# A convolution and soft mixture of experts on one core, rewritten: 64x64 tiles, block transposes on VectorE, and x in two halves

## The chip, the cores and the metric

The kernel runs on one core of a Trainium2 chip. The core has a matrix engine (TensorE, PE in the profile), a vector engine (VectorE, DVE), a scalar engine (ScalarE, ACT), GpSimd (POOL), and queues that start DMA transfers: SyncE's (SP) and, if a kernel uses it, ScalarE's. Inputs and output lie in HBM; the engines work on SBUF (128 partitions), and TensorE writes to PSUM (8 banks of 512 fp32 numbers per partition).

The metric is the device time of one execution in microseconds (us). Lower is better.

## The reference

Everything is fp32. With `x` of shape (8, 3584, 192), `weight` (8 heads, 7 taps), `phi` (192, 32), `w1` (8, 192, 1024) and `w2` (8, 1024, 192):

```python
w = softmax(weight)                       # per head, over the 7 taps
y[b, s, h, g] = sum_k w[h, k] * x_pad[b, s + k, h, g]   # causal, 6 zero rows in front, 24 channels a head
y = y.reshape(28672, 192)                 # N tokens
logits = y @ phi                          # (N, 32): 8 experts x 4 slots
d = softmax(logits over the N tokens)     # dispatch weights
slot_input = d.T @ y                      # (32, 192)
slot_out[e] = relu(slot_input[e] @ w1[e]) @ w2[e]       # 4 slots per expert
c = softmax(logits over the 32 slots)     # combine weights
out = c @ slot_out                        # (N, 192)
```

The dispatch softmax runs over all tokens, so no output row can be computed before all tokens have been read once. That makes three phases: convolution, logits and the sums over tokens; the experts; the combine. x is 22.0 MB, w1 and w2 are 6.3 MB each, the output is 22.0 MB.

## The kernel before, in words

**Tokens** are cut in two ways. Eleven "P" chunks hold tiles of 120 consecutive tokens on partitions. `conv_p` (matmul at L551) multiplies windows of 128 rows with a band matrix `toep` of 128 x 120, one matmul of 384 columns per head and 16 tiles; the result is copied from PSUM (banks `cv0`, `cv1`) to `xc` by ACT through the helper `copy` (L231 is its ACT branch, L233 its DVE branch). Four "D" chunks (the first 2048 tokens of four batches) hold 16 consecutive tokens per partition, loaded with a halo of 6 tokens as rows of 16.9 KB. `conv_d` convolves them without TensorE: ACT does the first tap (L589), DVE the other six of each head (L599).

**`stage_b`** takes each chunk through TensorE transposes (L634, L653; copied to `xt1`, `xt2`), logits in four column groups of 32 (L668, L672), the running maximum (L689, L694), logits turned back with tokens on partitions (L709), subtraction and exponential (L735, L763), and the dispatch product with four column groups (L790). Its sums are rescaled by the change of the maximum (L702) and accumulated in `sacc` (L817, L810). `epath` computes the combine softmax in `eall` per token (L833 to L849).

**Experts.** Sums of groups are merged (L1037), the first layer is L1083 and L1087, the ReLU L1097, the transposes L1107, the second layer L1129. Late w1 and w2 loads reuse buffers of x. The upper 64 rows of w1 are loaded two experts at a time onto 128 partitions (L907, `w1[2 * q : 2 * q + 2, P:D, :]`).

**Combine.** The weights are split in a high and a low part (L994), transposed in pairs of tiles (L1008), and multiplied with `st`, which is split likewise, in fp32r (L1187). `store` sends the result to HBM, P tiles as rows of 768 B (L1216), D chunks as rows of 6 KB (L1204).

**Order.** All steps are given to `Plan` with their reads, writes, costs and priorities. It list-schedules them over the engines by these costs and emits each engine's instructions in that order. All DMAs are issued from SP, in one order, and SP waits at an issue until its buffer is free:

```python
src = bass.AP(x.tensor, (b * S + s0 - HALO) * D, ap=[[D, P], [M * D, e - i], [1, D]])
nc.sync.dma_start(xv[:, i:e, :], src)
```

Of the kernel before, what the change touches and what calls it, by code (L numbers as in the profile page):

```python
# [10 lines left out]
F32R = mybir.dt.float32r  # L11
# [6 lines left out]
class Plan:  # L18
    """Collects steps in program order with the buffers they read and write, orders them by list
    scheduling over the engines (every dependency between two steps is kept), then emits them."""  # L20

    LAG = {"PE": 0.22, "ACT": 0.2, "DVE": 0.16, "DMA": 2.1, "POOL": 0.2}
    SELF = {"PE": 0.0, "ACT": 0.1, "DVE": 0.12, "DMA": 2.1, "POOL": 0.1}
    SWITCH = 0.15
    FILL = 1500.0
    SLIP = 0.05
    LOOK = {"PE": 0.05, "ACT": 0.12, "DVE": 0.12, "DMA": 0.0, "POOL": 0.0}

    def __init__(self):
        self.steps = []  # L30
        self.urgent = 0.0
        self.writer = {}
        self.readers = {}

    def add(self, fn, cost, reads=(), writes=(), prio=0.0, bias=0.15):
        i = len(self.steps)
        deps = set()
        for r in reads:
            if r in self.writer:
                deps.add(self.writer[r])  # L40
        for w in writes:
# [9 lines left out]
        self.steps.append((fn, cost, deps, prio, bias, self.urgent))  # L51
        return i

    def list_order(self, todo, out):
        n = len(self.steps)
        succ = [[] for _ in range(n)]
        miss = [len(s[2]) for s in self.steps]
        for i, s in enumerate(self.steps):
            for d in s[2]:
                succ[d].append(i)  # L60
        ready = [i for i in range(n) if miss[i] == 0 and i in todo]
        free = {e: 0.0 for e in self.LAG}
        est = [{e: 0.0 for e in s[1]} for s in self.steps]
        busy = {e: 0.0 for e in self.LAG}
        while ready:
            best = None
            for e in free:
                cands = []
                for i in ready:
                    cost = self.steps[i][1]  # L70
                    if e not in cost:
                        continue
                    s = max(free[e], est[i][e])
                    if len(cost) > 1:
                        f = s + cost[e] - (self.SWITCH if e == "ACT" else self.steps[i][4])
                        if any(max(free[o], est[i][o]) + cost[o] < f for o in cost if o != e):
                            continue
                    cands.append((s, i))
                if not cands:
                    continue  # L80
                lim = min(cands)[0]
                s, i = min(
                    ((s, i) for s, i in cands if s <= lim + max(self.LOOK[e], self.steps[i][5])),
                    key=lambda c: (self.steps[c[1]][3], c[1]),
                )
                key = (s, busy[e], i, e)
                if best is None or key < best:
                    best = key
            s, _, i, e = best
            busy[e] += self.steps[i][1][e]  # L90
            ready.remove(i)
            f = s + self.steps[i][1][e]
            free[e] = f
            out.append((s, i, e))
            for k in succ[i]:
                for o in est[k]:
                    lag = self.SELF[e] if o == e else self.LAG[e]
                    est[k][o] = max(est[k][o], f + lag)
                miss[k] -= 1
                if miss[k] == 0 and k in todo:  # L100
                    ready.append(k)
        return est, miss, succ

    def order(self):
        """First the steps that phases 1 and 2 wait for, by list scheduling; the others go into the gaps."""
        n = len(self.steps)
        out = []
        est, miss, succ = self.list_order({i for i in range(n) if self.steps[i][3] < self.FILL}, out)
        assert len(out) == sum(s[3] < self.FILL for s in self.steps)
        done = {i for _, i, _ in out}  # L110
        held = {e: sorted((t, t + self.steps[i][1][e]) for t, i, x in out if x == e) for e in self.LAG}
        ready = {i for i in range(n) if i not in done and miss[i] == 0}
        busy = {e: 0.0 for e in self.LAG}

        def fit(e, i):
            t, c, h = est[i][e], self.steps[i][1][e], held[e]
            k = max(0, bisect.bisect_left(h, (t, 0.0)) - 1)
# [5 lines left out]
        fits = {}  # L123
        while ready:
            best = None
# [1130 lines left out]
```

## Time and profile before

| | |
|---|---|
| median of 3 runs | 317.65 us (315.68 to 321.15) |
| span of the profiled execution | 314.0 us, first to last instruction |
| median less that span | 3.65 us |
| instructions | 5852 |
| TensorE clock granted, mean | 0.916 of full speed |
| moved by DMA | 60.55 MB, mean 193 GB/s |

The profile is of one execution. Its page gives busy time per engine, the span in 40 slices (a digit is the busy share in tenths), the chain of work that ended last, and groups of instructions by source line. A group's line reads: line, engine, operation, output<-input, shapes, count | busy us, mean ns of one | idle time before it and what ended it. A stage's line reads: from:to in us, length, then busy us (and instructions) of PE, PE weight loads, DVE, ACT and POOL, then the granted TensorE clock, the DMA share and GB/s. A line of the chain reads: start, us, what. A line of a timeline is the same with the engine's name; SPq is the queue of SP. PEld is TensorE loading weights. Busy time counts overlapping instructions of one group once.

### The profile page before, as it was taken

The page shows a single profiled execution, that of the slowest core. Times are in us where ns is not written, and L with a number is a line of the kernel's source. Part 1 is how long each engine was busy: PE and PEld are TensorE (multiplying, and loading weights), DVE is VectorE, ACT ScalarE, POOL GpSimd, SP SyncE. Part 2 cuts the span into 40 slices and gives each one's busy share as a digit, 9 for nine tenths or more (in the row PEclk, how much of TensorE's full clock was granted, in tenths as well). Part 3 has the DMA queues.
Part 4 walks back from the last instruction along what each step waited for, and adds up shares of the span by engine and source line. Part 5 has one row for each costly group of instructions (what it writes and reads, how often), then busy time and mean ns, then how long its engine had stood idle before and what let it go on. Part 6 is the DMA issues. An engine that isn't in the chain of part 4 may idle for free.

```text
span 314.0 us, 5852 instructions
## 1 busy us (share of the span) xinstructions
PE 251.1 (80%) x2189; PEld 173.9 (55%) x2189; DVE 216.6 (69%) x497; ACT 196.9 (63%) x468; POOL 10.5 (3%) x48
## 2 busy tenths in 40 slices
PE   5467979996999899999400699989999999897700
PEld 5233454564456456665200466655689999887600
DVE  3616597996999899999910078888899997821100
ACT  2365678684878698756400385664379997786620
POOL 6000000100010000000000000020000000000000
PEclk9596799999999999999855599999999999999975
DMA  6999997997039654311372951980039989899995
GB/s 185 205 257 210 235 327 277 243 232 204 1 97 275 157 153 140 106 51 54 102 163 82 365 167 45 316 243 2 2 105 253 296 228 313 259 259 305 299 317 186
DMA packets 55909, 60.55 MB, mean 193 GB/s; under 512 B 2154, under 2 KB 52810, under 8 KB 55370
## 3 DMA queue, kind: packets, MB, share of 16 engines
q1 hardware_dynamic: 55882, 60.19, 67.7%
q8 instruction: 17, 0.28, 0.4%
q14 instruction: 10, 0.08, 0.1%
HBM read 38.16 MB, written 22.02 MB: 192 GB/s over the span
## 4 chain that ended last, share of the span: by engine, by line
PE 42%; DMA 36%; DVE 6%; SPq 6%; ACT 3%; issue 1%; ACTq 0%; DVEq 0%
DMA xd<-in_x_dram 14%; DMA x<-in_x_dram 11%; DMA out_dram<-xc 11%; PE cv L551 9%; PE tr L634 5%; SPq L477 5%; DVE xcd L599 4%; PE sp L790 4%; PE cv L1187 3%; PE lt L668 3%; PE lt L672 2%; PE tr L653 2%; PE tr L1008 2%; PE sp L1129 2%; ACT xc L231 1%
## 5 line engine op out<-in xcount | busy, mean ns | idle before, releaser
L599 DVE SCALAR_TENSOR_TENSOR xcd<-xd,wb,xcd 128x384 f32<-128x384 f32 x192 | 105.2, 615 | 9.6 <-ACT xcd L589 9.3
L551 PE MATMUL cv<-x,toep 128*120 128x384 f32 x160 | 67.5, 531 | 33.8 <-DMA x<-in_x_dram 31.6
L231 ACT COPY xc<-cv 120x384 f32<-120x384 f32 (+3 forms) x132 | 58.2, 476 | 55.5 <-PE cv L551 47.2
L551 PEld LDWEIGHTS cv<-x,toep 128*120 128x120 f32 x160 | 26.5, 195 | 57.3 <-issue 40.0
L231 ACT COPY xt<-tr 128x480 f32<-128x480 f32 (+2 forms) x104 | 48.2, 514 | 13.4 <-PE tr L634 9.7
L689 DVE TENSOR_SCALAR_CACHE_REDUCE lts<-lt 128x480 f32<-128x480 f32 (+2 forms) x15 | 9.9, 657 | 31.6 <-PE lt L672 31.5
L634 PEld LDWEIGHTS tr<-ident,xc 120*128 120x128 f32 x172 | 19.6, 144 | 15.1 <-ACT xt L231 6.8
L634 PE MATMUL tr<-ident,xc 120*128 120x120 f32 x172 | 24.1, 277 | 4.3 <-ACT xt L231 4.3
L1187 PE MATMUL cv<-st,et 128*120 128x192 f32 (+1 forms) x160 | 21.7, 276 | 3.2 <-ACT xc L231 1.8
L589 ACT ACTIVATE xcd<-xd,wb 128x384 f32<-128x384 f32 x32 | 19.0, 648 | 7.8 <-DMA xd<-in_x_dram 7.8
L1187 PEld LDWEIGHTS cv<-st,et 128*120 128x120 f32 (+1 forms) x160 | 18.8, 187 | 4.4 <-ACT xc L231 2.2
L1008 PE MATMUL tr<-ident,xd 120*128 120x120 f32 (+1 forms) x118 | 17.3, 270 | 0.0
L790 PE MATMUL sp<-xc,dsb 120*32 120x193 f32 x344 | 16.3, 329 | 0.9 <-ACT dsb L763 0.9
L231 ACT CAST et<-tr 128x480 fp32r<-128x480 f32 (+1 forms) x26 | 15.4, 596 | 2.2 <-PE tr L1008 2.2
L668 PE MATMUL lt<-xt,phi 128*32 128x480 f32 (+2 forms) x120 | 16.0, 607 | 0.0
L672 PE MATMUL lt<-xt,phi 128*32 128x480 f32 (+2 forms) x120 | 15.9, 602 | 0.0
L790 PEld LDWEIGHTS sp<-xc,dsb 120*32 120x32 f32 x344 | 10.3, 109 | 7.6 <-ACT dsb L763 2.8
L1187 PE MATMUL lt<-st,et 128*120 128x192 f32 (+1 forms) x80 | 12.4, 278 | 2.5 <-ACT xc L231 1.9
L735 DVE TENSOR_TENSOR dsb<-ln,mbs 120x512 f32<-120x512 f32 (+2 forms) x16 | 9.6, 613 | 6.3 <-ACT mbs L231 6.1
L233 DVE CAST xd<-eall 120x256 fp32r<-120x256 f32 (+2 forms) x24 | 7.0, 290 | 9.5 <-PE tr L1008 9.4
L1008 PEld LDWEIGHTS tr<-ident,xd 120*128 120x128 f32 (+1 forms) x118 | 12.3, 140 | 1.5 <-issue 1.2
L994 DVE TENSOR_TENSOR xd<-eall,xd 120x256 fp32r<-120x256 f32 (+2 forms) x30 | 12.6, 418 | 0.7
(154 smaller groups left out, 407.4 us busy)
## 6 DMA issues: line engine op xcount, KB each, us to landing
x<-in_x_dram SPq DMA_DIRECT2D x14, 768.0 KB, 28.8
out_dram<-xc SPq DMA_DIRECT2D x13, 720.0 KB, 9.8
xd<-in_x_dram SPq DMA_DIRECT2D x4, 1848.0 KB
out_dram<-xc SPq DMA_DIRECT2D x8, 768.0 KB, 6.2
x<-in_moe_w_dram SPq DMA_DIRECT2D x4, 768.0 KB
w1a<-in_moe_w_dram SPq DMA_DIRECT2D x5, 512.0 KB, 8.8
xd<-in_moe_w_dram SPq DMA_DIRECT2D x4, 512.0 KB
out_dram<-xc SPq DMA_DIRECT2D x4, 450.0 KB
```

The source lines that it names most:

```text
L231: nc.scalar.copy(dst, src)
L477: nc.sync.dma_start(xv[:, i:e, :], src)
L551: nc.tensor.matmul(pv, toep[:, h, :], ch["x"][:, 0:nt, d0:d1], start=True, stop=True)
L589: nc.scalar.activation(o, xv[:, 0:nt, d0 : d0 + CG], AF.Copy, scale=wb[:, h * KT : h * KT + 1])
L599: nc.vector.scalar_tensor_tensor(out=o, in0=xv[:, k : k + nt, d0 : d0 + CG], scalar=wb[:, h * KT + k : h * KT + k + 1], in1=o, op0=ALU.mul ...
L634: nc.tensor.transpose(tv[:, g, 0:R], src, ident[0:R, 0:R])
L668: nc.tensor.matmul(lv[g * NS : (g + 1) * NS], phi1, v1[:, 0:C, g, 0:R], start=True, stop=False)
L672: nc.tensor.matmul(lv[g * NS : (g + 1) * NS], phi2[g % 2], v2[:, 0:C, g // 2, 0:R], start=False, stop=True)
L790: nc.tensor.matmul(ps["sp"][g * NS : (g + 1) * NS, 0:D1], dsb[0:R, c, g * NS : (g + 1) * NS], mv, start=(c == 0), stop=(c == C - 1),)
L994: nc.vector.tensor_tensor(out=eh.bitcast(F32R)[0:R, 0:n, 1, :], in0=ev, in1=eh[0:R, 0:n, 0, :], op=ALU.subtract)
L1008: nc.tensor.transpose(tv[:, i, 0:R], eh[0:R, 2 * i : 2 * i + 2, :, :].rearrange("p t a n -> p (t a n)"), ident[0:R, 0:R])
L1187: nc.tensor.matmul(po[0:R, u, 0:D], et[:, i, 0:R], st[u][v], start=(v == 0), stop=(v == 1))
```

## The change

The kernel is written anew; phases and mathematics stay.

- **Tokens:** each batch is 64 windows of 56 tokens, 32 in each half of the partitions. A window is 64 rows (6 of the window before it, two beyond its end). All tokens go through TensorE; the convolution by DVE and the D chunks are gone.
- **x** has two buffers `xs` of one batch each. The lower half is issued by SP, the upper half by ACT.
- **`conv`:** the band matrix is 64 x 64 on both halves; a head is four matmuls of 384 columns, one per 64x64 tile of the array, into two banks. One ACT copy of 768 elements per head moves it to `xc`.
- **`chain`:** six DVE transposes in 32x32 blocks (1024 elements each) make `xt`; 96 matmuls of 32x32 tiles (256 or 192 columns) make the logits of the batch in four banks; DVE takes the maximum and transposes the logits back (`tin`); ACT takes the exponential; eight PE transposes, two ACT copies, the dispatch product, the accumulation with the correction `al`.
- **`rows`** is the combine softmax, now with two passes and one sum on POOL. **`slots`** transposes the weights back with DVE into the freed `xc`.
- **Experts:** one fp32 pass as before; the weights' last 64 rows are loaded onto 64 partitions at a time (`w1b`); `w1a` has a buffer of its own, `w1b` and `w2` reuse `xs` and `xt`.
- **Combine:** plain fp32, contraction over 32 rows in four row groups, into four banks; evictions of up to 768 elements by ACT or DVE. Each partition holds 7 consecutive tokens of a quarter of a batch, so a store sends 5376 B per partition (1536 B and 768 B in the first batch).
- **`Plan`** is shortened: a list schedule for the first two phases, then the rest into the gaps.

The core of the new code:

```diff
+    def load_x(b):
+        def src(row0, rows, win0, wins):
+            return bass.AP(x.tensor, (base + T * win0 + row0) * D, ap=[[D, rows], [T * D, wins], [1, D]])
+        def low(e):
...
+            nc.sync.dma_start(xv[0:64, 1:NW, :], src(0, 64, 1, NW - 1))
+        def high(e):
+            if b < B - 1:
+                nc.scalar.dma_start(xv[64:128, :, :], src(0, 64, NW, NW))
...
+        add(low, dma(n), reads=[f"z{s}"], writes=[f"xs{s}l"], prio=b * 10 - 30)
+        add(high, dma(n), writes=[f"xs{s}h"], prio=b * 10 - 30)
...
+    def conv(b):
...
+            def mm(e, h=h, k=k):
+                for g in range(2):
+                    for hf in range(2):
+                        r = slice(64 * hf, 64 * hf + 64)
+                        nc.tensor.matmul(
+                            cv[k][64 * g : 64 * g + 64, hf, 0 : NI * CG].rearrange("p (i c) -> p i c", c=CG),
+                            toep[r, h, :],
+                            xs[s][r, g::2, h * CG : (h + 1) * CG],
+                            start=True, stop=True,
+                        )
...
+            add(ev, {"ACT": act(2 * NI * CG)}, reads=[f"cv{k}", "one"], writes=[xck[s][h]], prio=pr)
...
+    def chain(b):
...
+            def tr(e, k=k):
+                nc.vector.transpose(xt[:, k], xc[s][:, :, 1 + 32 * k : 33 + 32 * k])
...
+            def lmm(e, k=k):
+                for a in range(4):
+                    r = slice(32 * a, 32 * a + 32)
+                    n = 24 if a % 2 else 32
+                    for c in range(4):
+                        nc.tensor.matmul(
+                            lg[32 * c : 32 * c + 32, a, 0 : U * n].rearrange("p (u j) -> p u j", j=n),
+                            phi4[r, k, :],
+                            xt[r, k, U * c : U * c + U, 0:n],
+                            start=(k == 0), stop=(k == NB - 1), tile_position=(32 * a, 32 * c),
+                        )
...
+                nc.vector.tensor_reduce(out=nmr[:, b, odd : odd + 1], in_=lview(odd), axis=AX.XY, op=ALU.max, negate=True)
...
+                nc.scalar.activation(
+                    dT[:, :, odd::2, 0:n].rearrange("p u a j -> p a u j"),
+                    lview(odd).rearrange("p a (u j) -> p a u j", j=n), AF.Exp, bias=nm,
+                )
+            def tin(e, odd=odd, n=n, q0=q0):
+                nc.vector.transpose(
+                    eall[:, b, q0 : q0 + n // 2, :].rearrange("p (a k) m -> p a (k m)", a=2), lview(odd)
+                )
...
+            def disp(e, v=v):
+                for u in range(4 * v, 4 * v + 4):
+                    for c in range(4):
+                        nc.tensor.matmul(
+                            lg[32 * c : 32 * c + 32, 2, 0:D1], dn[:, u, 32 * c : 32 * c + 32], xc[s][:, U * c + u, :],
+                            start=(u == 0), stop=(u == U - 1),
+                        )
...
+    load_x(0)
+    load_x(1)
+    conv(0)
+    for b in range(B):
+        chain(b)
+        if b + 2 < B:
+            load_x(b + 2)
+        if b + 1 < B:
+            conv(b + 1)
...
+        load_w(
+            w1b[64 * a : 64 * a + 64], w1[a::2, P:D, :].rearrange("q p f -> p q f"), P * F * 8,
+            f"w1b{a}", ["xs0l", "xs0h"], 1020 + a,
+        )
...
+            def mm(e, qs=qs, banks=banks, cb=cb, k=k):
+                for q in qs:
+                    for c in range(4):
+                        r = slice(32 * c, 32 * c + 32)
+                        nc.tensor.matmul(
+                            banks[c][:, (q - k) * D : (q - k + 1) * D], cb[r, :, q], so[r, :],
+                            start=True, stop=True, tile_position=(32 * c, 0),
+                        )
...
+                    dst = bass.AP(out.tensor, (b * S + c * NQ) * D, ap=[[TQ * D, P], [1, TQ * D]])
+                    nc.sync.dma_start(dst, ob[:, c].rearrange("p q d -> p (q d)"))
-                        nc.vector.scalar_tensor_tensor(
-                            out=o,
-                            in0=xv[:, k : k + nt, d0 : d0 + CG],
-                            scalar=wb[:, h * KT + k : h * KT + k + 1],
-                            in1=o,
```

More of the change, by code (lines that the diff above doesn't have):

```diff
@@ L1 @@
-import bisect
 from contextlib import ExitStack
@@ L50, in add, with order @@
         deps.discard(i)
[L51 to L55, printed above, removed]
+        self.steps.append((fn, cost, deps, prio))
+    def order(self):
+        S = self.steps
+        n = len(S)
         succ = [[] for _ in range(n)]
-        miss = [len(s[2]) for s in self.steps]
-        for i, s in enumerate(self.steps):
+        for i, s in enumerate(S):
             for d in s[2]:
                 succ[d].append(i)
[L61 to L94, printed above, removed]
-            for k in succ[i]:
[L96 to L102, printed above, removed]
@@ L104, in order @@
-    def order(self):
-        n = len(self.steps)
-        out = []
[L108 to L117, printed above, removed]
+        prio = [s[3] for s in S]
@@ L164, in order @@
+        run({i for i in range(n) if prio[i] < self.FILL}, False)
+        done = {i for _, i, _ in out}
+        run({i for i in range(n) if i not in done}, True)
         assert len(out) == n
         out.sort()
-        self.end = max(b for h in held.values() for _, b in h)
-        self.trace = [(s, e, self.steps[i][1][e], self.steps[i][3]) for s, i, e in out]
         return out
@@ new lines, in tile_conv_softmoe, with selector @@
+    add(c1, {"POOL": 3.0}, writes=["one", "dT", "s1z", "s2z", "z1"], prio=-90)
+    add(lambda e: nc.gpsimd.memset(hz, 0.0), {"POOL": 2.2}, writes=[f"hz{q}" for q in range(4)], prio=-20)
+    def phi_load(e):
+        for a in range(4):
+            nc.sync.dma_start(phi4[32 * a : 32 * a + 32], phi.rearrange("(k p) n -> p k n", p=32))
+    add(phi_load, {"DMA": 0.5}, writes=["phi4"], prio=-25)
+    def selector(e):
+        nc.vector.tensor_reduce(out=gsel[:, 0:NS], in_=ident.rearrange("p (g n) -> p n g", n=NS), axis=AX.X, op=ALU.add)
@@ new lines, in tile_conv_softmoe, with merge @@
+    for b in range(B):
+        rows(b)
+    for b in range(B):
+        slots(b)
+    pr = 300
+    pv4 = lambda t: t.rearrange("p (q a i) -> p q a i", a=2, i=SPE)
+    nmf = nmr[:, B, 2:3]
+    add(
+        lambda e: nc.tensor.matmul(cv[0][:, 0, 0:P], nmf.broadcast_to((P, P)), ident, start=True, stop=True),
+        {"PE": 0.25}, reads=[f"nm{B - 1}", "ident"], writes=["cv0"], prio=75.5,
+    )
+    def merge(e):
+        nc.vector.tensor_reduce(
+            out=gmin, in_=cv[0][:, 0, 0:P].rearrange("p (g n) -> p n g", n=NS), axis=AX.X, op=ALU.min
+        )
+        nc.vector.tensor_tensor(out=gtmp, in0=gmin, in1=gsel[:, 0:NS], op=ALU.mult)
+        nc.vector.tensor_reduce(out=gcol, in_=gtmp, axis=AX.X, op=ALU.add)
@@ L1126, in l2 @@
+                    copy(e, hz[:, 2 * q : 2 * q + 2, x_, x_ * SPE : (x_ + 1) * SPE], tv[:, :, c_ : c_ + SPE])
+            return fn
+        add(hcopy(0), {"DVE": 0.4}, reads=[f"ht{q % 2}", f"hz{q}"], writes=[f"hz{q}a"], prio=pr + 3)
+        add(hcopy(1), {"ACT": 0.8}, reads=[f"ht{q % 2}", f"hz{q}"], writes=[f"hz{q}b"], prio=pr + 3)
+        op = lg[:, 2, 0:D]
+        def l2(e, q=q):
+            for j in range(2):
                 for a in range(2):
@@ new lines, in l2 @@
+                            start=(q == 0 and j == 0 and a == 0), stop=(q == 3 and j == 1 and a == 1),
+                        )
+        add(
+            l2, {"PE": 1.4}, reads=[f"hz{q}a", f"hz{q}b"] + [f"w2.{e}" for e in range(E)],
+            writes=["op"], prio=pr + 1.5,
+        )
+    add(
+        lambda e: nc.vector.tensor_scalar(out=os_, in0=op, scalar1=ri, scalar2=None, op0=ALU.mult),
+        {"DVE": 0.35}, reads=["op", "ri"], writes=["os"], prio=pr + 4,
+    )
+    add(
+        lambda e: nc.tensor.matmul(lg[:, 3, 0:D], gsel, os_, start=True, stop=True),
+        {"PE": 0.35}, reads=["os", "gsel"], writes=["lg1"], prio=pr + 4,
+    )
```

1223 lines of the change are left out of this document (377 added, 846 removed).

## The prediction

> **What bounds the kernel now.** I read the page from the top: the span, the busy shares, then the forty slices, because a mean over stages hides which engine sets each.
>
> ```profile
> span 314.0 us, 5852 instructions
> ...
> PE 251.1 (80%) x2189; PEld 173.9 (55%) x2189; DVE 216.6 (69%) x497; ACT 196.9 (63%) x468; POOL 10.5 (3%) x48
> ...
> DMA  6999997997039654311372951980039989899995
> ```
>
> No engine is full over the span, and the DMA row has a hole from the 10th slice to the 30th and is full again at the end. So I asked for stages (busy time of PE, weight loads, DVE, ACT, POOL; clock, DMA share, GB/s).
>
> ```profile
> 80.00:100.00 20.00, 20.00 (x167) 11.18 (x166) 19.93 (x42) 16.24 (x37) 1.36 (x3) 1.00 0.48 118
> 100.00:120.00 20.00, 18.96 (x174) 11.60 (x173) 18.41 (x39) 16.36 (x40) 0.00 (x0) 1.00 0.54 150
> 130.00:140.00 10.00, 10.00 (x107) 6.03 (x108) 9.97 (x22) 7.00 (x18) 0.12 (x1) 1.00 0.13 53
> 160.00:180.00 20.00, 4.58 (x18) 3.38 (x19) 0.00 (x0) 2.02 (x4) 0.00 (x0) 0.52 0.70 211
> 240.00:248.00 8.00, 8.00 (x78) 8.00 (x77) 7.76 (x21) 7.78 (x19) 0.00 (x0) 1.00 0.97 315
> 296.00:302.00 6.00, 1.92 (x16) 1.75 (x16) 0.00 (x0) 3.54 (x9) 0.00 (x0) 1.00 0.99 360
> 302.00:310.00 8.00, 0.00 (x0) 0.00 (x0) 0.00 (x0) 0.00 (x0) 0.00 (x0) 0.50 0.94 282
> ```
>
> Three limits follow one another. From 80 to 140 us PE and DVE are both full while DMA is half idle or worse: compute sets the pace. From 130 the queue moves only 53 GB/s at a share of 0.13, two engines of sixteen: the four late loads of w1, whose access pattern begins with a dimension of 2. The x behind them in the same queue is late, and from 160 to 180 everything waits for it. From 240 on the stores fill the DMA. The end of the chain of waits shows the three parts:
>
> ```profile
> 213.45 0.43 DVE saccD L810
> 222.28 1.44 PE sp L1129 x32
> 230.19 1.16 PE cv L1187 x7
> ```
>
> Sums over tokens end at 213.9, experts until 230.2 (16.3 us), combine until 314 (84 us).
>
> **The change, part by part.**
>
> *What goes.* The convolution by DVE, its largest group, and the PE transposes for the logits with their ACT evictions:
>
> ```profile
> L599 DVE SCALAR_TENSOR_TENSOR xcd<-xd,wb,xcd 128x384 f32<-128x384 f32 x192 | 105.2, 615 | 9.6 <-ACT xcd L589 9.3
> L231 ACT COPY xt<-tr 128x480 f32<-128x480 f32 x63 | 33.2, 570 | 8.0 <-PE tr L634 7.2 <-PE tr L653 0.7
> ```
>
> DVE loses 105 us. The 53 GB/s loads go too: the new w1b loads begin with 64 partitions. What is late next must be summed per batch (3584 tokens, eight of them), since all four resources now do the same work eight times.
>
> *DVE per batch.*
>
> ```profile
> L386 DVE TENSOR_REDUCE eall<-eall 128x152 f32<-128x1064 f32 x1 | 1.3, 1261 | 0.0
> L833 DVE TENSOR_REDUCE rmr<-eall 120x16 f32<-120x512 f32 x10 | 6.8, 680 | 0.0
> L817 DVE SCALAR_TENSOR_TENSOR saccP<-saccP,small,sp 128x193 f32<-128x193 f32 x9 | 3.6, 405 | 0.3 <-PE sp L790 0.2
> L845 DVE RECIPROCAL rmr<-rmr 120x16 f32<-120x16 f32 x10 | 2.5, 253 | 0.3
> L844 DVE TENSOR_SCALAR rmr<-rmr 120x16 f32<-120x16 f32 x10 | 1.7, 175 | 0.3
> ```
>
> The first two give 1.05 ns an element and 0.14 fixed. Six block transposes of 1024 elements: 6 x 1.22 = 7.3, if a transpose goes as a reduction does; no row shows one. Bounds: half (as if two elements went at once) and three times. I take one, the pace of every row here. Two maxima from PSUM (512 and 384): 0.68 + 0.55 = 1.2. Transposing the logits back: 1.2. Minimum and accumulation: 0.6. Row maximum of 896: 1.1, reciprocal 0.4. Sum 11.8. The transposes back for the combine (about 1.4 a batch, 11 in all) can't run before the convolved tiles have been read for the last time; they fall beside the experts, where DVE is nearly free. POOL takes two passes of 896 elements and a sum tree, some 2700 elements:
>
> ```profile
> L1074 POOL MEMSET xt<- 128x2048 f32 x1 | 1.8, 1814 | 22.1 <-PE lt L668 22.1
> ```
>
> At 0.89 ns an element that is 2.4 us; at four times that it still fits, and nobody waits for it before the combine.
>
> [...]
>
> *ACT per batch.*
>
> ```profile
> L231 ACT COPY xc<-cv 120x384 f32<-120x384 f32 x97 | 46.2, 503 | 50.0 <-PE cv L551 44.0 <-DMA out_dram<-xc 4.7 <-PE cv L1187 0.7
> L231 ACT COPY eall<-ln 120x512 f32<-120x512 f32 x10 | 5.8, 585 | 0.0
> L840 ACT ACTIVATE eall<-eall 120x512 f32<-120x512 f32 x10 | 6.4, 638 | 2.7 <-DVE eall L837 2.7
> L702 ACT ACTIVATE small<-small 128x1 f32<-128x1 f32 x12 | 3.5, 295 | 1.0 <-DVE small L694 1.0
> ```
>
> Eight evictions of 768 now go to ACT alone: 0.78 each by the slope, 6.2. Exponentials 512 and 384: 1.1; two copies of 512: 1.2; correction 0.3; row exponential of 896: 0.95. Sum 9.8. Added: ACT issues the upper half of each x load.
>
> ```profile
> 54.97 1.99 SPq L477 DMA_DIRECT2D x<-in_x_dram  x2
> 11.12 5.02 SPq L477 DMA_DIRECT2D x<-in_x_dram  x2
> ```
>
> An issue takes 1.0 us with a short queue and 2.5 behind a full one. The ACT queue holds one earlier half at most, so I take 1.0: 10.8. The issue also waits for the convolution two batches back to have read the buffer; behind it in ACT's order stand the exponentials and evictions for the next batch. The last eviction needs that same convolution's last matmul, so the wait costs about one eviction at worst. The lower half waits the same way on SP; only w1 loads stand behind it.
>
> *PE per batch.*
>
> ```profile
> 45.80 0.65 PE cv L551 x2
> 47.27 0.94 PE lt L668 x8
> 110.32 1.44 PE sp L790 x32
> 44.98 0.82 PE tr L634 x8
> ```
>
> 384 columns take 0.33 us; eight matmuls of 480 columns in four column groups take 0.94, so the groups run side by side, about 1 ns a column. The change adds row groups, and no row shows these side by side. If they are: convolution 8 x 0.33, logits 6 x 0.25, transposes 0.82, dispatch 1.44, sum 6.4. If the row groups queue: 8 x 0.65 + 6 x 0.88 + 2.3 = 12.8. I take the middle, 9.6, as column groups do run so; both ends lie under the period below.
>
> *x loads.* One batch is 64 rows x 64 windows x 768 B = 3.15 MB (25.2 in all).
>
> ```profile
> 108.00:114.00 6.00, 4.96 (x54) 3.19 (x52) 5.51 (x11) 6.00 (x15) 0.00 (x0) 1.00 0.90 262
> 10.00:20.00 10.00, 6.65 (x15) 3.12 (x16) 3.06 (x10) 4.62 (x13) 0.00 (x0) 0.74 0.96 206
> 172.00:176.00 4.00, 0.58 (x1) 0.47 (x2) 0.00 (x0) 0.00 (x0) 0.00 (x0) 0.50 0.99 383
> 4.97 16.68 DMA xd<-in_x_dram
> ```
>
> In the first row two loads of 768 B pieces over 128 partitions pass alone: 262 GB/s at a share of 0.90, 290 when full. That is 10.8 us a batch, provided that the two halves together run as one whole did. The other bounds are 206 (15.3 us) and 383 (8.2 us). One w1 load of 0.52 MB per batch adds 1.5: 12.3.
>
> *Period and sum.* DMA 12.3, DVE 11.8, ACT 10.8, PE about 9.6: nearly level. The old order kept its full engine 95 to 100% busy, so 12.3 / 0.95 = 13.0. The first load lands at about 14 us (10.8 plus issue and landing), in whose shadow the band matrix is built. Seven periods, 91. The last batch needs its convolution and transposes (8), its logits (2), and the chain maximum, exponential, transpose, eviction, dispatch, accumulation (0.7 + 0.6 + 0.2 + 1.1 + 0.8 + 0.6 + 1.4 + 0.4 and handovers: 7): 17. End of the sums: 122, against 213.9.
>
> Experts: the same chain as before, 16.3. New is that five w2 loads go into buffers free only after the last convolution, three only after the last logits: 5.5 MB after about 112 us, at 360 to 383 GB/s 15 us, landed near 130. The second layer asks for them some 9 us after 122. They are just hidden; I add 1.7. Combine starts at 140. Were the cover gone, each microsecond shows in full.
>
> Combine: per batch 28 x 192 columns in row groups, 4.5 to 9 us of PE even with the groups queued at full or half clock, and 5376 elements of eviction shared by ACT and DVE, about 3 us. Stores: 22.0 MB, in pieces of 5.4 KB instead of mostly 768 B. The two last windows of the second fence price both: 360 GB/s where 6 KB pieces go out, 282 with 768 B alone. At 360, 61 us. First store 2 us after the start, 2 to land. 140 + 2 + 61 + 2 = 205. The profiled span is 314.0 and the median of three runs 317.65, so 3.65 lies around it: 208.7, **209 us**. Of the 109 us gained, 92 come before 214, 19 from the stores, less 2 in the experts.
>
> **The rivals.**
>
> *The halves don't add up.* If x comes at 206 GB/s, the lowest full-share row, a batch costs 15.3 + 1.5 = 16.8; the period is 16.8 and the first load 4.5 later: 7 x 3.8 + 4.5 = 31 more, **240 us**. For it: 206 is a measured rate, and each half reaches only half the partitions. Against it: the rate of 290 with the same pieces, and that the 206 belongs to a D chunk's long rows, under way from 5.0 to 21.7 by the last row of that fence. [...] No run here shows halves.
>
> *Row groups queue, or ACT stalls at the issue.* PE at 12.8, broken by waits on single logit banks, or ACT at 10.8 + 1.5 to 4: a period near 15, 14 more, **223 us**. For it: the 2.5 us issue row; against: short own queue.
>
> *Block transposes are slow.* At two cycles an element DVE has 20.3 a batch: 7 x 7.3 + 7 = 58 more, **267**. At three cycles, 28.8, plus 22 for the transposes back that no longer hide beside the experts: 209 + 7 x 15.8 + 10 + about 10 = **340, slower than before**. It decides from about 2.8 cycles. For it: no transpose in this trace. [...]
>
> **How the numbers follow.** Forecast 0.55, halves 0.22, queueing or stalls 0.13, transposes at two cycles 0.06, at three or more 0.04. The range: below, no loss in order (period 11.8) and stores at 383 GB/s, 209 - 8 - 4 - 2 = 194; above, the halves rival with stores at 300 GB/s, 240 + 12 = 252. It leaves the slow transposes out. From these cases faster by over 2%, 0.94; within, 0.01; slower, 0.05. Two per cent is about what measuring this kernel can tell from no change.
>
> **What would show it.** Right: DVE transposes of 1024 near 1.22 us; conv evictions near 0.78; DMA share near 0.9 and 260 to 290 GB/s from 5 to 110 us; last accumulation near 122; stores at 360 GB/s from about 142 to the end, ended by DMA. Wrong: long "PE cv <- DMA xs" waits with 200 GB/s at full share (halves), PE full with row groups one after the other, ACT issues over 2 us, or transposes over 2 us. The sum is weakest where four resources lie within 20%: waits between them could cost more than the 5% taken.

## The result and the profile after

The new kernel takes 295.2 us (median of 4 runs, 293.6 to 297.9) against 317.5: ratio 0.932, 95% interval 0.923 to 0.940. It is faster, but 86 us slower than the forecast of 209 and outside the range. The profiled execution took 295.5 us, its span is 293.7. Executions of one kernel differed by 1.5% here and by 3.4% in a later set (seven of the kernel before, 313.2 to 324.0 us); the ratios leave out those more than 1.5% above the fastest of their kernel.

The page's span and DMA row:

```profile
span 293.7 us, 7488 instructions
DMA  6979999999869989949979659249700089999996
```

Three stages, in the columns of the prediction's fences (PE, weight loads, DVE, ACT, POOL; clock, DMA share, GB/s):

```profile
10.00:20.00 10.00, 0.00 (x0) 0.00 (x0) 3.34 (x9) 0.84 (x4) 0.00 (x0) 0.50 0.99 191
60.00:130.00 70.00, 53.68 (x1084) 24.37 (x1060) 34.16 (x47) 28.39 (x42) 15.99 (x20) 0.90 0.88 170
250.00:260.00 10.00, 8.09 (x96) 7.03 (x92) 4.53 (x7) 5.65 (x8) 0.00 (x0) 0.87 1.02 409
```

While both halves of x load and PE waits for them (10 to 20 us), the queue is full at 191 GB/s. In the middle, nothing is full over the stretch: DMA 0.88, PE 54 of 70 us. The stores run at 409. The chain of waits gives the ends of the phases:

```profile
211.46 0.64 PE cv L619 x2
222.30 1.48 PE lg L699 x32
232.88 1.25 PE cv L742 x16
```

Sums end at 211 (before: 213.9), experts at 232.9 (230.2), combine at 293.7 (314). **The whole gain is the combine: 61 us instead of 84. The first phase, rewritten for 92 us of gain, brought 3.** The clearest gauge of that phase is the accumulation, once a batch:

```profile
L482 DVE COPY acc<-lg x1: 322/322/322, 57.9 to 57.9; 128x193 f32<-128x193 f32 x1
L478 DVE SCALAR_TENSOR_TENSOR acc<-acc,small,lg x7: 374/376/417, 83.1 to 211.0; 128x193 f32<-128x193 f32 x7
```

The first sum starts at 57.9, the eighth at 211.0: 153.1 / 7 = 21.9 us a batch, where 13.0 was forecast. The groups behind it (busy us, mean ns | idle before and what ended it):

```profile
L398 DVE STREAM_TRANSPOSE xt<-xc 128x1024 f32<-128x1024 f32 x48 | 56.9, 1219 | 39.9 <-ACT xc L181 39.8
L181 ACT COPY xc<-cv 128x768 f32<-128x768 f32 x64 | 51.5, 817 | 85.7 <-PE cv L370 77.6 <-issue 8.1
L370 PE MATMUL cv<-xs,toep 64*64 64x384 f32 x512 | 66.1, 599 | 33.2 <-DMA xs<-in_x_dram 20.7 <-ACT xc L181 9.2 <-issue 3.0
L408 PE MATMUL lg<-xt,phi 32*32 32x192 f32 (+1 forms) x1536 | 38.0, 377 | 13.7 <-issue 13.6
L469 PE MATMUL lg<-xc,dn 128*32 128x193 f32 x512 | 28.1, 366 | 6.0 <-ACT dn L181 6.0
L455 PE MATMUL lg<-ident,dT 128*128 128x128 f32 x64 | 12.3, 323 | 10.2 <-ACT dT L434 9.4 <-ACT dn L181 0.7
```

DVE and ACT cost what the prediction said. PE doesn't: 66.1 + 38.0 + 28.1 + 12.3 = 144.5 us, 18.1 a batch instead of 9.6. And the logits' matmuls stood still for 13.6 us before "issue", that is, while they waited for nothing that the profile shows. What that wait is became the main question.

### The profile page after: what moved, and what is told of

It reads as the page before. It is cut to its first block, busy times and chain, and to the rows that moved or that the text cites. A ratio compares the mean times of both kernels' runs of the same rounds, so it can differ in the third digit from the quotient of the medians.

```text
span 293.7 us, 7488 instructions
## 1 busy us (share of the span) xinstructions
PE 200.9 (68%) x3346; PEld 112.0 (38%) x3346; DVE 134.2 (46%) x229; ACT 109.2 (37%) x180; POOL 53.4 (18%) x73
## 4 chain that ended last, share of the span: by engine, by line
PE 53%; ACT 11%; DMA 8%; issue 8%; DVE 7%; SPq 5%; ACTq 3%; POOL 1%; DVEq 0%
PE cv L370 14%; PE lg L408 11%; PE lg L469 10%; DMA xs<-in_x_dram 8%; PE cv L742 6%; PE lg L742 5%; SPq L349 4%; ACT dT L434 3%; PE lg L455 3%; DVE eall L440 3%; ACTq L252 3%; ACT xc L181 2%; DVE nmr L419 2%; ACT xs L181 2%; ACT dn L181 2%
## 5 line engine op out<-in xcount | busy, mean ns | idle before, releaser
L370 PE MATMUL cv<-xs,toep 64*64 64x384 f32 x512 | 66.1, 599 | 33.2 <-DMA xs<-in_x_dram 20.7
L181 ACT COPY xc<-cv 128x768 f32<-128x768 f32 x64 | 51.5, 817 | 85.7 <-PE cv L370 77.6
L398 DVE STREAM_TRANSPOSE xt<-xc 128x1024 f32<-128x1024 f32 x48 | 56.9, 1219 | 39.9 <-ACT xc L181 39.8
L408 PE MATMUL lg<-xt,phi 32*32 32x192 f32 (+1 forms) x1536 | 38.0, 377 | 13.7 <-issue 13.6
L370 PEld LDWEIGHTS cv<-xs,toep 64*64 64x64 f32 x512 | 19.3, 153 | 64.3 <-issue 34.4
L510 POOL TENSOR_TENSOR eall<-eall,rms 128x896 f32<-128x896 f32 x16 | 26.9, 1696 | 72.4 <-ACT xc L181 54.2
L742 PE MATMUL cv<-so,xc 32*128 32x192 f32 x256 | 29.2, 476 | 6.5 <-ACT xs L181 4.2
L408 PEld LDWEIGHTS lg<-xt,phi 32*32 32x32 f32 x1536 | 19.6, 105 | 35.8 <-issue 25.5
L469 PE MATMUL lg<-xc,dn 128*32 128x193 f32 x512 | 28.1, 366 | 6.0 <-ACT dn L181 6.0
L419 DVE TENSOR_REDUCE nmr<-lg 128x1 f32<-128x512 f32 (+1 forms) x16 | 9.2, 620 | 45.8 <-PE lg L408 45.8
L742 PEld LDWEIGHTS cv<-so,xc 32*128 32x128 f32 x256 | 23.0, 317 | 10.2 <-ACT xs L181 6.1
L742 PE MATMUL lg<-so,xc 32*128 32x192 f32 x192 | 21.1, 466 | 2.6 <-DVE xs L185 1.6
L455 PE MATMUL lg<-ident,dT 128*128 128x128 f32 x64 | 12.3, 323 | 10.2 <-ACT dT L434 9.4
L742 PEld LDWEIGHTS lg<-so,xc 32*128 32x128 f32 x192 | 17.4, 320 | 4.2 <-DVE xs L185 2.1
L181 ACT COPY dn<-lg 128x512 f32<-128x512 f32 x16 | 9.4, 585 | 22.3 <-PE lg L469 21.4
L455 PEld LDWEIGHTS lg<-ident,dT 128*128 128x128 f32 x64 | 7.9, 159 | 22.6 <-ACT dT L434 14.0
## 6 DMA issues: line engine op xcount, KB each, us to landing
w1a<-in_moe_w_dram SPq DMA_DIRECT2D x8, 512.0 KB, 13.1
xt<-in_moe_w_dram SPq DMA_DIRECT2D x3, 768.0 KB, 12.8
```

Source lines behind the costliest of these rows:

```text
L181: nc.scalar.copy(dst, src)
L370: nc.tensor.matmul(cv[k][64 * g : 64 * g + 64, hf, 0 : NI * CG].rearrange("p (i c) -> p i c", c=CG), toep[r, h, :], xs[s][r, g::2, h * CG ...
L398: nc.vector.transpose(xt[:, k], xc[s][:, :, 1 + 32 * k : 33 + 32 * k])
L408: nc.tensor.matmul(lg[32 * c : 32 * c + 32, a, 0 : U * n].rearrange("p (u j) -> p u j", j=n), phi4[r, k, :], xt[r, k, U * c : U * c + U, 0:n],
L419: nc.vector.tensor_reduce(out=nmr[:, b, odd : odd + 1], in_=lview(odd), axis=AX.XY, op=ALU.max, negate=True)
L455: nc.tensor.transpose(lg[:, v, u * P : (u + 1) * P], dT[:, 4 * v + u].rearrange("p a j -> p (a j)"), ident)
```

## The experiments

All start from the new kernel. Times are medians of two to four executions; the ratio is to the kernel before. "Spacing" is the mean distance of the eight accumulations; "idle at issue" is PE's idle time put down to issue before logits and conv matmuls (the two figures after `<-issue` in the L408 and L370 groups, 16.6 in the kernel); "packet" is the mean time of x's 768-byte packets in the trace.

| | time us | ratio (95%) | first, last sum | spacing | idle at issue | packet ns |
|---|---|---|---|---|---|---|
| the kernel | 295.2 | 0.932 (0.923 to 0.940) | 57.9, 211.0 | 21.9 | 16.6 | 67.9 |
| 1 both halves on SP | 294.0 | 0.933 (0.916 to 0.949) | 57.8, 207.5 | 21.4 | 13.9 | 69.4 |
| 2 one transfer over 128 partitions | 262.4 | 0.834 (0.823 to 0.845) | 43.7, 179.2 | 19.4 | 7.4 | 41.2 |
| 3 half of x from batch 2 on | 270.8 | 0.863 (0.855 to 0.870) | 57.0, 186.4 | 18.5 | 8.0 | 63.1 |
| 4 half of logits and dispatch | 267.8 | 0.853 (0.833 to 0.874) | 54.3, 184.3 | 18.6 | 2.7 | 68.9 |
| 5 2 and 4 together | 215.3 | 0.680 (0.674 to 0.687) | 38.2, 130.2 | 13.1 | 0 | 41.2 |
| 6 idle loads | 298.2 (295.5, 300.8) | - | 56.4, 213.0 | 22.4 | 25.0 | 69.8 |
| 7 as 6, without these loads | 270.3 | 0.857 (0.847 to 0.867) | 56.9, 184.6 | 18.2 | 2.9 | - |
| 8 w1a behind x | 286.7 | 0.910 (0.905 to 0.916) | 56.3, 201.5 | 20.7 | 12.7 | 69.9 |
| 9 as 8, few short transfers queued | 284.9 | 0.905 (0.897 to 0.914) | 61.0, 197.0 | 19.4 | 5.2 | 58.2 |

**1. Both halves on SP.**

```diff
-        add(low, ...)    # SP
-        add(high, ...)   # nc.scalar.dma_start
+        add(lowhigh, ...)    # low(e), then high(e) with nc.sync.dma_start
```

> Edit: both halves of a batch's x are issued by SP, one behind the other, in one step as soon as the buffer is free; bytes, pieces and the two half-partition transfers stay. Rate theory (a half of the partitions loads at 184-191 GB/s whichever queues carry it, so phase 1 needs 25.2 MB / 188 GB/s = 134 us of loading): the share and the rate in a loading window stay at 184-191 GB/s; only the 5 to 17 us by which the upper half is issued late go, so the queue has no gaps: last x landed at about 155 instead of 165, sums end near 200, time 283-290. Order theory (the late issue on ACT costs about 10 us per batch): sums end at 170 or earlier, time under 260. Theory that two queues are what makes the halves slow together: rate rises over 250 GB/s. PE theory (18.5 us of PE per batch sets the period): no change, 293-297.

294.0, and 188 GB/s from 10 to 20 us (191 with two queues): the late issue of the upper half on ACT isn't the cause, nor are two queues.

**2. One transfer over 128 partitions.** The upper half gets wrong rows.

```diff
+            nc.sync.dma_start(xv[:, :, :], src(0 if b else ZS, 128, 0, NW))
```

> Edit: x of a batch in one transfer over all 128 partitions from SP, same number of bytes and of 768-byte pieces; rows 64 to 127 of each window get the rows that follow the first 64 instead of the second half of the sequence, so the sums are of other data. Beside the kernel with both halves on SP it differs only in how many partitions one transfer spans. Rate theory: 290-400 GB/s in a loading window, x of a batch in 8-11 us instead of 17; if the rate of the halves alone bounds phase 1, sums end at about 150-160 (period 13-14), time 235-245. PE theory: loads finish early, but sums end at 8 x 18.5 + 20 + tail, some 185-200, time 270-285. Order theory: about the same as with both halves on SP.

The stage in which these loads run nearly alone, and one from the middle of phase 1:

```profile
5.00:15.00 10.00, 1.58 (x10) 1.39 (x9) 7.91 (x19) 1.54 (x6) 0.15 (x1) 0.71 1.08 336
60.00:130.00 70.00, 58.84 (x1296) 27.90 (x1296) 41.58 (x58) 35.73 (x52) 24.35 (x28) 0.97 0.59 177
```

336 GB/s instead of 191 (188 in experiment 1) at a full queue, with pieces of the same size: here the span of a transfer, 128 partitions against 64, set the rate. The rival of the prediction, that halves don't add up, is true of the rate: both together reach 191 GB/s. But the time is 262, not the 235 to 245 that the rate alone would give: with the queue at 0.59, PE is busy 58.8 of 70 us at nearly full clock (0.97). Behind the loads stands PE. Of the 33 us gained, 14 come before the first sum (43.7 instead of 57.9).

**3. Half of x from batch 2 on.** The other windows keep an earlier batch's rows.

```diff
-            nc.sync.dma_start(xv[0:64, 1:NW, :], src(0, 64, 1, NW - 1))
+            m = NW if b < 2 else NW // 2     # and so for the upper half
+            nc.sync.dma_start(xv[0:64, 1:m, :], src(0, 64, 1, m - 1))
```

> Edit: from batch 2 on only the first 16 of 32 windows of each half are loaded; the others keep the rows of an earlier batch, so 10 MB of 25 are left out and the sums are of other data. Issue places and order are unchanged. Rate theory: loading per batch 8.5 us instead of 17, sums end near 160, time about 245. PE theory (18.5 us of PE per batch at full clock, over 20 with the clock granted): sums end at 190-205, time 275-290. Order theory: the gain is in between, and PE keeps idle gaps before conv matmuls while no x is in flight.

270.8. By single accumulations, batches 2 to 5 follow at 17.3, 17.3, 17.3 and 17.4 us: as will be seen, PE's own pace.

**4. Half of the logits and of the dispatch left out.**

```diff
-        for k in range(NB):
+        for k in range(NB // 2):
-                for u in range(4 * v, 4 * v + 4):
+                for u in range(4 * v, 4 * v + 2):
```

> Edit: three of the six row blocks of the logits and half of the dispatch matmuls are left out (112 of the some 250 fp32 matmuls of a batch; about 5.3 us of PE per batch, 42 us over the phase); all else stays, the sums are of less. Rate theory: sums end within 5 us of 211, time 288-296. PE theory: sums end near 170-180, time 255-265. Order theory (the chain of one batch is waited for): sums end some 10-25 us earlier.

267.8, near the PE theory's figure, and yet now the loads bind: conv waits for x 42.0 us in this run (20.7 in the kernel) and spacing stays at 18.6.

**5. Both, 2 and 4.**

> Edit: the two leave-outs together: x of a batch in one transfer over 128 partitions (wrong rows in the upper half), and half of the logits and dispatch matmuls left out. Alone they brought 33 and 27 us. If loading and PE are the two limits that phase 1 runs against in turn (17 us and some 18.5 us of each per batch, 19.4 per batch with the quick transfer, 18.6 with fewer matmuls), both together bring the sum or more: period 13 to 15 us, last sum at 145-150, time about 225-235. If what is left is the order of the program and the chain of one batch, the period stays over 17 and the time over 245.

215.3, below the 225 to 235 expected. Its accumulations, and a stage from the middle of phase 1:

```profile
L484 DVE COPY acc<-lg x1: 322/322/322, 38.2 to 38.2; 128x193 f32<-128x193 f32 x1
L480 DVE SCALAR_TENSOR_TENSOR acc<-acc,small,lg x7: 374/375/418, 51.2 to 130.2; 128x193 f32<-128x193 f32 x7
60.00:100.00 40.00, 34.76 (x620) 15.35 (x620) 31.30 (x42) 27.66 (x43) 8.93 (x13) 1.00 0.89 267
```

(130.2 - 38.2) / 7 = 13.1 us a batch, the forecast's 13.0. With x at the rate that it had assumed (267 GB/s at a share of 0.89, 300 when full) and PE's work under its period (34.76 of 40 us), the forecast's period holds; the first sum is still late, 38.2 where 31 was forecast. Alone they bring 33 and 27 us, together 80: each hides the other.

**The planner's costs.**

```diff
-{"PE": 0.66}  {"PE": 0.46}  {"PE": 0.45}  {"PE": 1.36}  dma(n)
+{"PE": 0.75}  {"PE": 1.25}  {"PE": 0.8}   {"PE": 1.7}   dma(2 * n)
```

> Edit: nothing but the costs that the planner is told: conv 0.75 instead of 0.66 us, one set of logits 1.25 instead of 0.46, transposes 0.8 instead of 0.45, half a dispatch 1.7 instead of 1.36, each half of x at 175 instead of 350 GB/s, so that the order on PE and the place of the issue on ACT follow what the trace measured. Order theory: gaps go, 270-283. Rate and PE theory: within 5 us of 295, since the order of a list scheduler with priorities by batch hardly moves.

295.9: nothing. The wrong costs in the schedule aren't the reason.

**Window by window.** An attempt at right data over 128 partitions.

```diff
+                return bass.AP(x.tensor, (base + T * win) * D, ap=[[NW * T * D, 2], [D, 64], [1, D]])
...
+            for w in range(1, m):
+                q.dma_start(xv[:, w, :], two(w))    # q is nc.sync
```

> Edit: the right data in transfers that span 128 partitions: window by window, both halves in one transfer of 128 pieces of 768 bytes, 31 or so issues on SP per batch instead of one large transfer for each half. Rate theory, if a transfer's span over the partitions is what counts: packets of 768 bytes fall from 68 to about 41 ns, but SP has about 35 issues of 0.6 us per batch, 21 us, so the loading is bound by issue at 150-160 GB/s and the time stays at 285-300; if an issue of a small transfer takes only 0.3 us, 262-275. If the rate hangs on the number of pieces or on the source's order and not on the span, packets stay at 68 ns.

699.8, 2.2 times the kernel before; no theory had that. A stage of it:

```profile
100.00:140.00 40.00, 0.00 (x0) 0.00 (x0) 0.00 (x0) 0.00 (x0) 0.00 (x0) 0.50 0.14 44
```

44 GB/s at a share of 0.14, that is 2.2 engines of sixteen. The access pattern begins with a dimension of 2, as the late w1 loads of the kernel before, which the prediction read at 53 GB/s and 0.13: the prediction itself had read the warning. The packets took 39.5 ns, about as with one transfer over 128 partitions (41.2). A pattern with the 64 ahead of the 2 wasn't tried.

**No loads of x from batch 2 on.**

```diff
+        if b > 1:
+            return
```

> Edit: x is loaded for the first two batches alone; the later ones compute on those rows, with every other instruction and the order as in the kernel. It shows what phase 1 costs without the loads. If PE's 18.5 us per batch is the other limit, the batches follow at 18 to 19.5 us and the time is 260-270; if the loads were the whole loss, they follow at 13 and the time is about 215-225. PE's idle stretches at the borders of 256 instructions, 16 us in all in the kernel, should shrink under 6 us if the loads in flight hold up the fetch of PE's instructions.

277.7 (274.4 and 280.9), spacing 18.4: without any load of x from batch 2 on, phase 1 is PE's, and still far from 13. Of the time idle at issue 6.9 us are left, where under 6 was expected; 4.3 of them fall beside the late loads of weights.

**Conv ahead of the chain,** with both halves on SP; then also with w1a behind the last x, then with the measured costs as well.

```diff
-        s, pr = b % 2, b * 10        # conv
+        s, pr = b % 2, b * 10 - 6
```

> Edit: both halves issued by SP, and the conv of the next batch put ahead of the chain of the present one in the planner's priorities, so that the buffer of x comes free some 10 us earlier and the next load starts while the one before is still in flight. Beside the kernel with both halves on SP alone (294). Theory that both limits add because a load can't start before a conv that is stretched over the chain: period falls from 21.4 to 18-19.5, time 272-284. Theory that PE and loads are near their limits anyway: within 5 us of 294.

> Edit: as the one with conv ahead of the chain, and the eight loads of w1a (4.2 MB, some 16 us of the queue) put behind the last x on SP instead of among the loads of x. If the queue is the limit until the last x (landed at 165 of 294), the last x lands 10-16 us earlier, sums end 8-14 us earlier, and the experts wait for weights by at most a few us: time 8-14 us under the version with w1a among the loads. If the two batches behind the last load (46 us of PE) or the weights set the end, no gain or a loss of up to 8.

> Edit: as the one with w1a behind the last x, with the planner's costs as measured (conv 0.75, logits 1.25, transposes 0.8, half a dispatch 1.7, x at 175 GB/s). The costs alone brought nothing in the kernel as it was (295.9). Expected: within 4 us of the version with the old costs.

306.5, 302.4 and 305.6: all slower than 294. In the second, spacing is 23.2 and the idle time at issue 18.1. Starting the loads earlier made phase 1 longer, against every theory on the table. The second differs from version 8 below (286.7) in the priority alone. Between the first and the last sum PE stands still for 45.8 us in it and for 31.7 in version 8. Of these 14 us more, 5.4 are the unexplained wait, and 9.6 are waits of the chain for ACT and DVE (before transposes and logits).

**6. Loads that nobody waits for.** Both halves on SP as in 1; from batch 2 on they go to the buffer of w1a (loaded behind them); conv reads the first two batches' rows.

```diff
-        xv = xs[s]
+        xv = xs[s] if b < 2 else w1a[...]     # 24 KB of its 32 per partition
-        add(lowhigh, ..., writes=[f"xs{s}l", f"xs{s}h"])
+        add(lowhigh, ..., writes=[... if b < 2 else "xd"])
```

> Edit: the loads of x for batches 2 to 7 go on, in halves and both from SP, but into the buffer of w1a, which is loaded behind them; conv computes on the first two batches' rows and waits for no later load. Beside the kernel without these loads (batches follow at 18.4 us) it differs only in the traffic. If the full queue itself slows PE (fetch of its instructions), batches follow at 20 to 20.8 while the queue is full, and PE stands still for 10 us or more in all at the borders of 256 instructions; if only conv's waits for x cost time, they follow at 18.2 to 18.8.

**7. The same without these loads,** with the same order of the compute engines in phase 1.

> Edit: the version with loads that no conv waits for, without those loads (x of batches 2 to 7 isn't loaded at all); the order of the engines in phase 1 is the same. Fetch theory: the batches follow at 17.3 to 18 us from the second on, no stall over 1 us at a border of 256 instructions between 60 and 140 us, sums end some 20-28 us earlier than with the idle loads (213). If the fetch isn't it and the order made those 25 us, it stays at 22 and more.

298.2 (295.5 and 300.8) against 270.3 (269.0 and 271.6). The middle of phase 1, with the idle loads:

```profile
60.00:130.00 70.00, 47.48 (x849) 19.70 (x852) 28.04 (x39) 24.76 (x37) 12.17 (x14) 0.83 1.11 195
```

and without them:

```profile
60.00:130.00 70.00, 58.52 (x1280) 28.21 (x1270) 42.24 (x57) 38.10 (x56) 20.53 (x25) 0.98 0.01 2
```

The logits' group, with and without:

```profile
L411 PE MATMUL lg<-xt,phi 32*32 32x192 f32 (+1 forms) x1536 | 38.2, 386 | 15.4 <-issue 15.4
```

```profile
L411 PE MATMUL lg<-xt,phi 32*32 32x192 f32 (+1 forms) x1536 | 33.7, 368 | 0.0
```

This is the sharpest pair. Nothing in phase 1 waits for the idle loads, yet in the same 70 us PE does 849 matmul records beside them and 1280 without them. Single batches follow at 24.7 and 26.1 us while they run, and at 17.3 and 17.5 without them. PE stands still, and it works more slowly as well (386 ns for a record of the logits against 368), while the clock granted is lower (0.83 against 0.98). Two of the stops on PE's timeline with the idle loads:

```profile
71.30 1.10 PE L411 MATMUL lg<-xt,phi 32*32 32x192 f32 x21 [5.75 <-issue]
91.10 1.07 PE L411 MATMUL lg<-xt,phi 32*32 32x256 f32 x13 [4.16 <-issue]
```

Counting PE's records (matmuls and weight loads) with the idle loads from the start, the five stops of over 2 us between the first sum and 140 us come at record 951, 1207, 1719, 2487 and 2999: steps of 256, 512, 768 and 512. The table of queues on that page shows what comes in such blocks:

```profile
q8 instruction: 26, 0.43, 0.7%
```

26 transfers of 16 KB for PE's 6692 records, one per 256 or so; experiment 4, with 4644 records, has 18. By their times in the trace, each of the five stops ends 1.4 to 1.7 us after one of them has landed (the block behind the stop that ends at 71.30 was moved from 68.2 to 69.6). **So the stops are read as PE waiting for its own instructions, which come by DMA as x does:** the page's table has both, each as a share of the same 16 engines (q8 0.7%). With next to no loads hardly any stop is left (2.9 us in experiment 7, one stop beside the late loads of weights), and in experiment 5 none, though the queue is busy at 0.89. So it isn't a busy queue alone that does it. In experiment 5 a packet takes 41.2 ns instead of 69.8, so the same loads stand in the queue for less time; that this is the difference is argued.

**8. w1a behind the last x,** with both halves on SP, then in the kernel as it is.

```diff
-        load_w(w1a[:, e, :], ..., f"w1.{e}", [], 1001 + e)
+        load_w(w1a[:, e, :], ..., f"w1.{e}", [], 1001 + e, ["xs1l", "xs1h"])
```

> Edit: both halves from SP, and w1a behind the last x instead of among the loads; priorities as in the kernel. Beside the kernel with both halves on SP (294): x of batch 1 lands some 8 us earlier and the first sum comes at 48-52 instead of 57.8; the queue has 16 us less to do up to the last x. If that is worth its time: 278-288. If the chain and PE take it back behind the last x or the experts wait for w1a: 290-297.

> Edit: the kernel as it is, the upper half on ACT's queue, with w1a alone behind the last x. Expected as for the version with both halves on SP, within 5 us of it: 278-297; the late issue of the upper half stays.

286.7 and 287.0 (ratio 0.904, 0.892 to 0.915). The first sum comes only 1.5 us earlier than in 1 (56.3, where 48 to 52 was expected), but w1a's 4.2 MB no longer stand among the loads. This is 7 to 8 us, 2 to 3%, under the kernel and under experiment 1 (0.905 to 0.916 lies below both intervals), and the simplest version here that beats both kernels.

**Half of the combine's stores left out.**

```diff
-            for c in range(4):
+            for c in range(2):      # stores of batches 1 to 7
```

> Edit: for batches 1 to 7 the stores of the third and fourth quarter of the rows are left out, matmuls and evictions stay. If the stores bound the combine (61 us, 22 MB at 411 GB/s), it becomes as long as what PE and the evictions need, which the busy shares (PE 80%, DVE 45-57%) put at some 45-50 us: time 280-285. If PE or the evictions bound it, it stays at 61 and the time at 293-297. Phase 1 is untouched.

282.3. The combine starts at 233.6 and ends with the span at 280.7: 47 us instead of 61. The stores bound it.

**9. A shallow queue,** on version 8: transfers of 8 windows, then of 4. Reloading one row of the last low transfer makes SP wait until that has landed (24 waits, 76.5 us with 8 windows), so two short transfers stand in the queue, or three for a moment.

```diff
+            for w in range(0, NW, G):    # G is 8, then 4
+                if w:
+                    nc.sync.dma_start(xv[32:33, w - 1 : w, :], src(32, 1, w - 1, 1))
...
+                nc.sync.dma_start(xv[0:64, a : w + G, :], src(0, 64, a, w + G - a))
...
+                nc.sync.dma_start(xv[64:128, w:m, :], src(0, 64, NW + w, m - w))
```

> Edit: on the version with w1a behind the last x (286.7). x of a batch goes in eight transfers of 8 windows, low and high by turns; ahead of each next low transfer one row of 768 bytes of the last one is loaded again, so that SP waits until that one has landed: not more than two transfers (0.79 MB, 4.2 us) stand in the queue. Theory that the fetch of instructions stands behind what was queued before it: PE's stalls at the borders of 256 instructions fall from 12-16 us to under 6, batches follow at 18.5 to 19.5, time 272-280. Theory that the traffic itself slows the fetch: stalls as before, and the loading somewhat slower: 286-296.

> Edit: the same with transfers of 4 windows: at most 0.39 MB, 2.1 us, in the queue. If depth decides: stalls under 3 us, but gaps in the loading of about 1 us per pair of transfers, so that a load takes 20 us or more: 275-290. If depth doesn't decide: 290-300.

284.9 and 344.2. The middle of phase 1 and the logits' group with transfers of 8 windows:

```profile
60.00:130.00 70.00, 59.48 (x1231) 27.59 (x1223) 39.91 (x54) 31.81 (x46) 19.95 (x22) 0.93 0.76 158
```

```profile
L407 PE MATMUL lg<-xt,phi 32*32 32x192 f32 (+1 forms) x1536 | 35.6, 363 | 2.5 <-issue 2.4
```

and of 4:

```profile
60.00:130.00 70.00, 47.82 (x844) 20.94 (x847) 28.70 (x37) 26.11 (x38) 7.81 (x9) 0.82 0.45 119
```

```profile
L407 PE MATMUL lg<-xt,phi 32*32 32x192 f32 (+1 forms) x1536 | 38.7, 418 | 0.6 <-issue 0.6
```

The stops go, from 8.1 us before the logits' matmuls in version 8 to 2.4 and 0.6. That fits a fetch held up by what stands in the queue ahead of it; with a short one it mostly comes in time, at a DMA share of 0.76. With 8 windows the traffic hardly falls (158 GB/s; version 8 moves 165 in this stretch), but the busy share does (0.94 in version 8), so depth isn't quite parted from it. The times miss what was expected (272 to 280, and 275 to 290), because with a shallow queue x also came more slowly (160 and 99 GB/s from 10 to 20 us, 188 in experiment 1). With 8 windows the first sum comes 4.7 us later than in version 8, which takes back half of the 9.2 us that the spacing gains, and the ratio (0.897 to 0.914) isn't clear of version 8's. With 4, at 119 GB/s, conv waits 83.4 us for x.

## Why the prediction was wrong, step by step

Sums were to end at 122 and ended at 211; everything behind them was to take 83 us (122 to 205) and took 82.7. The whole error of 89 us lies in phase 1: 27 us until the first sum (57.9, where 122 less seven periods gives 31) and 62 in the spacing (7 x 8.9).

**PE's term was half of what it is: the failed step.** The prediction read `0.65 PE cv L551 x2` as two matmuls of 384 columns and `1.44 ... x32` as 32. In the trace an fp32 matmul is two records: the new code issues 8 x 4 x 8 = 256 convolution matmuls and L370 counts x512. So 0.65 was one matmul, and the dispatch product, forecast at 1.44, takes 28.1 / 8 = 3.5: the old row holds 16 matmuls, and a batch now has 32. What the prediction doubted, tiles side by side, isn't the error:

```profile
57.49 1.52 PE L370 MATMUL cv<-xs,toep 64*64 64x384 f32 x16
```

Sixteen records are two heads at the full clock, 0.76 for a head's four 64x64 tiles, little more than one matmul of 128 rows. The logits, 16 small tiles per set, cost 38.0 / 8 = 4.75 instead of 1.5. Sum 18.1; in experiment 7, at a higher clock, 16.9. "Both ends lie under the period" failed with it: the upper bound, 12.8, was built from the same misread rows.

**x's term: the rival was right about the rate, not about how it acts.** 290 GB/s was conditional on "the two halves together run as one whole did". They run at 191; 3.15 MB take 16.5 us, not 10.8. The rival named it, at 0.22, with 240 us. It missed the time, since it left PE at 9.6, far under its period of 16.8; and the loads don't set the period as it had thought. PE waits for x only twice in the kernel (in total, times, longest), both before the first sum, ending at 20.2 and 43.4 us; behind it the loads act through PE's stops and slower work (15 and 10 us in all, below):

```profile
PE cv L370 <- DMA xs<-in_x_dram: 20.7, 2, 14.2
```

**The step from the terms to the period failed too.** "12.3 / 0.95" had the old kernel's coupling, whose full engine wasn't starved. Here PE without the loads (experiment 7) gives a spacing of 18.2, 5.2 over the forecast or 36 us in seven; with the loads it is 21.9, another 26. Between the first and the last sum PE stands still for 39.0 us in the kernel and 23.8 in experiment 7, and is busy for 113.8 and 103.7 with equally many records. So 15 of the 26 are standing still and 10 are slower work, at a mean clock of 0.87 against 0.94 in these stretches. In them the idle time at issue is 13.9 against 2.9, and 7.8 is one wait that the second rival foresaw, an issue on ACT behind a full queue with the evictions behind it:

```profile
151.68 7.46 ACTq L252 DMA_DIRECT2D xs<-in_x_dram  x1
160.84 1.56 PE L370 MATMUL cv<-xs,toep 64*64 64x384 f32 x8 [7.76 <-ACT xc L181]
```

Without ACT's issues, in experiment 1, the last sum comes only 3.5 us earlier. That the clock makes the 10 us is worked out, not shown by itself: 113.8 / 103.7 = 1.10, and 0.94 / 0.87 = 1.08.

**The start** (31 forecast, 57.9): the first conv begins at 20.2 instead of 14; the conv of batch 1, in PE's order ahead of the rest of the first chain, waits 6.5 us for its x (the row below); and PE needs nearly twice the time that the sum had given it.

```profile
43.43 2.83 PE L370 MATMUL cv<-xs,toep 64*64 64x384 f32 x14 [6.51 <-DMA xs<-in_x_dram]
```

**Right:** the block transposes, 1219 ns for 1024 elements (1.22; the rivals at two and three cycles, a cycle being the reductions' 1.05 ns an element, are out), conv evictions 817 ns (780), ACT's issues 0.60 us where the queue had room (1.0 was taken), POOL waited for only once behind the start (0.6 us), and the combine: stores at 409 GB/s rather than 360, 61 us where 65 were forecast. The experts took 21.4 us instead of 18.

**Open:** what decides whether the fetch comes late; the time that the queued loads take would fit these runs, but it wasn't varied alone. And a version that has x over 128 partitions with the right data: by experiment 2 it is worth some 30 us, more than all else tried here.

## What to carry to other kernels

Check what one record of a trace is before pricing with it: divide a group's count by the number of instructions the code issues. When several resources come out level, don't add a few per cent: halve the demand on each in turn and on two together, since here either alone gave 34 to 41% of the gain of both. And a full, deep DMA queue may not be free for PE even if nothing waits for its data (here 849 matmul records in 70 us beside such loads, 1280 without): stops "<-issue", here at steps of 256 records, are the sign.

## What the runs showed of the hardware

- While loads filled the queue, PE stood still for 2 to 6 us at a time, at steps of 256 records or a multiple, each time until 1.4 to 1.7 us after a 16 KB block of instructions had landed (25.0 us idle at issue in all with the idle loads; 2.9 us without them, 5.2 and 0.6 with few short transfers queued). None came in experiment 5, with the queue busy at 0.89 by transfers over 128 partitions.
- A 768-byte packet took 68 to 70 ns in transfers over 64 partitions with a deep queue, 41.2 over 128; with a shallow queue 58.2 and 45.6 over 64.
- An fp32 matmul is two matmul and two weight-load records on TensorE (L370: 256 issued, x512 of each); a transpose is one of each (L455: 8 a batch, x64). Four 64x64 tiles ran side by side (0.76 us for four times 384 columns, 0.65 for one matmul of 128 rows in the kernel before).
